# Attention and SwiGLU block on one core: VectorE's weight joins moved to the end of a slot, thresholds and a scaling moved to ScalarE

## The chip, the cores and the metric

One core of a Trainium2 chip. The metric is the time of one execution on the device in microseconds (us). The kernel before took 1633.53 us (median of 3 runs, 1629.41 to 1633.9).

## The reference

```python
# q, k, v: (8 batches, 8 heads, 576, 64);  weights: double precision, 512x1536 twice and 1536x512
scores = scale * q @ k.T
thresh = max(scores, axis=-1) - tau
scores = where(scores >= thresh, scores, -1e9)
attn   = exp(scores - max(scores));  attn /= sum(attn) + 1e-9
x      = (attn @ v) rearranged to (4608, 512)
g      = x @ w_gate
out    = (g * sigmoid(g) * (x @ w_val)) @ w_out
```

## The kernel before

The program is a sequence of *slots*. A slot is one row tile of a pair of heads: scores on TensorE, row maxima (`nm`), threshold (`th`), exponentials, masked products with their sums (`p`), a scaling by the reciprocal sums (`ri`). Slots 1 to 20 are batch one, the rest batches two to eight (`halved`: the same work in halves of 288 columns and a transpose on VectorE). Beside the attention of a slot, `fill` gives TensorE pieces of the feed-forward part from slot 13 on.

The weights come in double precision, in 24 pieces. ScalarE splits a piece into a high and a low half, four VectorE operations put sign, exponent and the high half together, and two GpSimd products add the low half. From the third slot on, each slot joins one piece, so the joins end in the sixth slot of batch two.

```python
def join_weights():
    ...
    nc.vector.tensor_scalar(out=up, in0=up, ..., op0=ALU.min, op1=ALU.max)                        # L169
    nc.vector.tensor_scalar(out=ub, in0=ub, ..., op0=ALU.logical_shift_left, op1=ALU.bitwise_and) # L171
    yield
    nc.vector.scalar_tensor_tensor(out=ub, in0=hi, ..., in1=ub, ...)                              # L174
    nc.vector.tensor_scalar(out=ex.bitcast(U32), in0=ub, ..., op0=ALU.bitwise_and)                # L176
    nc.gpsimd.tensor_tensor(out=lo, in0=lo, in1=ex, op=ALU.mult)                                  # L178
    nc.gpsimd.tensor_tensor(out=up, in0=up, in1=lo, op=ALU.add)                                   # L179

def scores(seg, t):
    ...                                    # matmuls, row maxima nm
    if halved:
        nc.scalar.activation(th[:, 0:m], nm[:, 0:m], AF.Identity, bias=cut, scale=-1.0)           # L300
    else:
        nc.vector.tensor_scalar(out=th[:, 0:m], in0=nm[:, 0:m], ...)                              # L302
    for x in range(m):
        nc.scalar.activation(ps[x], scs[x], AF.Exp, bias=nm[:, x:x + 1])                          # L304
    yield
    ...                                    # transposes of an earlier slot
    for x in range(m):
        nc.vector.scalar_tensor_tensor(out=ps[x], in0=scs[x], scalar=th[:, x:x + 1], in1=ps[x],
                                       op0=ALU.is_ge, op1=ALU.mult, accum_out=...)                # L308
    ...                                    # sums, reciprocal ri (L316)
    yield
    for x in range(m):
        if halved:
            nc.gpsimd.tensor_scalar(out=ps[x], in0=ps[x], scalar1=ri[:, x:x + 1], ...)            # L320
        else:
            nc.scalar.activation(ps[x], ps[x], AF.Copy, scale=ri[:, x:x + 1])                     # L322
    ...

# the slot loop, cut
    go = scores(seg, t); next(go)
    ...
    if n or x:
        weights()            # fetch, first half of the join (L169, L171), split the next piece
    next(go)                 # masked products, sums, reciprocal
    finish_weights()         # second half of the join (L174, L176) and GpSimd's products
    fill(part)
    next(go)                 # scaling of p
    if len(unsig) >= SIG:
        sigmoids()           # three sigmoids, three GpSimd products (L466)
    fill(part)
    ...
    if x == len(seg["tiles"]) - 2 and n + 1 < len(segs):
        prepare(segs[n + 1])                 # transposes of q and k
        fetch_qk(segs[n + 1]["i"] + 1)       # loads of q and k, scaling of q on GpSimd (L220)
```

## Time and profile before

| part of the run | length | what bounds it |
|---|---|---|
| 22 to 103 us, slots 3 to 12, ten joins | 81 us | VectorE |
| 103 to 166 us, rest of batch one | 63 us | TensorE |
| 166 to 240 us, last slot of batch one and six of batch two, last seven joins | 74 us | VectorE |
| from 310 us on | 1320 us | TensorE |

The lines that carry this, with the busy times, are in the prediction below. A line of a group gives source line, engine, operation, tiles and shapes, count, busy us and mean ns of one, and the idle time of the engine in front of it with what ended it. A line of a timeline gives start and duration in us. A record (the stretch of time that the profile gives one instruction) can contain a wait that counts as busy: the same threshold instruction takes 0.61 us in the trace of before and 0.23 us in the first experiment below, at the same place in VectorE's order.

### The profile page before, as it was taken

What the parts mean: (1) busy time and instruction counts of PE and PEld (TensorE: products, weight loads), DVE (VectorE), ACT (ScalarE), POOL (GpSimd) and SP (SyncE); (2) the same over time, 40 slices, a digit from 0 to 9 for tenths busy, and PEclk for the clock granted to TensorE, in tenths of its full rate; (3) what the DMA queues carried; (4) which work ended last, traced back from release to release, by engine and by line L of the source; (5) the groups of instructions that cost most, each with busy time, mean ns of one, the idle gap of its engine ahead of it and who ended that gap; (6) DMA issues with size and microseconds to landing.
All of it is one profiled execution on the core that took longest, in us unless ns stands there. A gap on an engine that the chain in (4) does not pass through costs nothing.

```text
span 1629.5 us, 27646 instructions
## 1 busy us (share of the span) xinstructions
PE 1554.5 (95%) x10192; PEld 835.1 (51%) x10192; DVE 1102.8 (68%) x3680; ACT 571.3 (35%) x1248; POOL 790.9 (49%) x704
## 2 busy tenths in 40 slices
PE   6889779989999999999999999999999999999998
PEld 4555444558545455455545545455545545555453
DVE  7987988777787787777767777767767777601000
ACT  5666532333424323333323423324324323302011
POOL 3543776565455545645545645545555645402011
PEclk9799989999999999999999999999999999999999
DMA  6532221111111111110111111110111110000000
GB/s 160 130 104 98 68 69 37 43 30 37 30 43 30 43 37 22 31 38 20 30 43 37 30 43 36 36 30 20 25 43 37 30 49 16 8 13 0 13 6 20
DMA packets 176342, 66.67 MB, mean 41 GB/s; under 512 B 159568, under 2 KB 159568, under 8 KB 176208
## 3 DMA queue, kind: packets, MB, share of 16 engines
q1 hardware_dynamic: 173328, 55.47, 15.0%
q0 software_dynamic: 2880, 9.44, 1.5%
q8 instruction: 81, 1.33, 0.3%
q14 instruction: 53, 0.43, 0.1%
HBM read 55.44 MB, written 9.44 MB: 40 GB/s over the span
## 4 chain that ended last, share of the span: by engine, by line
PE 79%; DVE 14%; issue 3%; ACT 2%; POOL 1%; DMA 1%; SPq 0%; DVEq 0%; POOLq 0%; ACTq 0%
PE pg L447 20%; PE pv L455 20%; PE po L480 19%; PE sc L268 8%; PE xa L403 8%; DVE p L308 3%; DVE mx L288 2%; DVE p L334 1%; PE sc L273 1%; DVE mx L245 1%; DVE wgv L169 1%; PE xa L375 1%; POOL p L320 1%; DVE nm L298 1%; ACT L304 1%
## 5 line engine op out<-in xcount | busy, mean ns | idle before, releaser
L320 POOL TENSOR_SCALAR p<-p,ri 128x288 f32<-128x288 f32 x504 | 498.4, 1004 | 440.3 <-DVE ri L316 436.5
L447 PE MATMUL pg<-xT,wgv 128*128 128x384 f32 (+1 forms) x1248 | 403.4, 466 | 4.0 <-ACT gt L448 4.0
L455 PE MATMUL pv<-xT,wgv 128*128 128x384 f32 (+1 forms) x1248 | 406.3, 469 | 0.0
L480 PE MATMUL po<-wo,ht 128*128 128x512 f32 x864 | 387.2, 600 | 1.2 <-POOL ht L466 1.2
L455 PEld LDWEIGHTS pv<-xT,wgv 128*128 128x128 f32 x1248 | 231.2, 192 | 152.6 <-issue 17.5
L447 PEld LDWEIGHTS pg<-xT,wgv 128*128 128x128 f32 x1248 | 228.5, 190 | 156.8 <-issue 20.6
L308 DVE SCALAR_TENSOR_TENSOR p<-sc,th,p 128x288 f32<-128x288 f32 (+1 forms) x540 | 257.0, 528 | 39.8 <-ACT p L304 39.4
L480 PEld LDWEIGHTS po<-wo,ht 128*128 128x128 f32 x864 | 160.4, 191 | 207.0 <-issue 195.4
L304 ACT ACTIVATE p<-sc,nm 128x288 f32<-128x288 f32 (+1 forms) x540 | 236.0, 511 | 32.1 <-DVE nm L298 31.5
L288 DVE TENSOR_REDUCE mx<-sc 128x2 f32<-128x576 f32 x252 | 179.5, 749 | 91.7 <-PE sc L268 91.4
L300 ACT ACTIVATE th<-nm,cut 128x4 f32<-128x4 f32 (+1 forms) x140 | 41.6, 297 | 563.2 <-DVE nm L291 563.2
L268 PE MATMUL sc<-kT,qT 64*32 64x288 f32 x4032 | 174.2, 417 | 34.4 <-DVE p L308 34.4
L456 DVE TENSOR_TENSOR ht<-gt,pv 128x384 f32<-128x384 f32 (+1 forms) x156 | 78.3, 510 | 177.9 <-PE pv L455 172.4
L334 DVE STREAM_TRANSPOSE p<-p 128x576 f32<-128x576 f32 x252 | 181.3, 753 | 0.8 <-POOL p L320 0.8
L466 POOL TENSOR_TENSOR ht<-ht,gt 128x768 f32<-128x768 f32 (+1 forms) x78 | 130.4, 1701 | 95.0 <-ACT gt L465 92.4
L268 PEld LDWEIGHTS sc<-kT,qT 64*32 64x32 f32 x4032 | 67.4, 107 | 144.4 <-issue 111.9
L448 ACT COPY gt<-pg 128x384 f32<-128x384 f32 (+1 forms) x156 | 70.6, 458 | 186.0 <-PE pg L447 181.9
L403 PE MATMUL xa<-p,vall 64*64 64x288 f32 x2016 | 132.1, 409 | 2.0 <-ACT gt L448 1.9
L403 PEld LDWEIGHTS xa<-p,vall 64*64 64x64 f32 x2016 | 77.2, 134 | 59.1 <-issue 15.0
L245 DVE TENSOR_REDUCE sums<-sums 32x4 f32<-32x4 f32 (+1 forms) x560 | 83.9, 150 | 10.5
L418 DVE COPY xT<-xa 128x96 f32<-128x96 f32 (+1 forms) x56 | 14.5, 295 | 112.2 <-PE xa L403 112.1
L245 DVE TENSOR_REDUCE mx<-mx 32x4 f32<-32x4 f32 (+1 forms) x560 | 83.1, 148 | 10.4
(72 smaller groups left out, 918.6 us busy)
## 6 DMA issues: line engine op xcount, KB each, us to landing
vall<-in_v_dram SPq DMA_DIRECT2D x112, 144.0 KB, 3.2
qraw<-in_q_dram SPq DMA_DIRECT2D x128, 72.0 KB, 2.3
kraw<-in_k_dram SPq DMA_DIRECT2D x128, 72.0 KB, 2.7
out_dram<-ob POOLq DMA_DIRECT2D x36, 256.0 KB, 2.4
wo<-in_moe_w_gate_dram SPq DMA_DIRECT2D x16, 384.0 KB, 3.5
wo<-in_moe_w_val_dram SPq DMA_DIRECT2D x16, 384.0 KB, 4.0
xT<-in_moe_w_out_dram SPq DMA_DIRECT2D x6, 768.0 KB, 5.8
wo<-in_moe_w_out_dram SPq DMA_DIRECT2D x2, 768.0 KB, 4.4
```

The lines of the kernel that those rows point to most:

```text
L245: nc.vector.tensor_reduce(out=x[g * G:(g + 1) * G, 0:m, 1], in_=x[o * G:(o + 1) * G, 0:m, 0:1], axis=AX.X, op=ALU.max)
L268: nc.tensor.matmul(ps[g * G:(g + 1) * G, u, 0:SH], qT[hs, col + a * G:col + (a + 1) * G], kT[hs, c * SH:(c + 1) * SH], start=True, stop=True)
L288: nc.vector.tensor_reduce(out=mx[:, 2 * x:2 * x + 2, 0], in_=tile_[:, :, 0:SH], axis=AX.X, op=ALU.max, negate=True)
L304: nc.scalar.activation(ps[x], scs[x], AF.Exp, bias=nm[:, x:x + 1])
L308: nc.vector.scalar_tensor_tensor(out=ps[x], in0=scs[x], scalar=th[:, x:x + 1], in1=ps[x], op0=ALU.is_ge, op1=ALU.mult, accum_out=sm[:, x, ...
L320: nc.gpsimd.tensor_scalar(out=ps[x], in0=ps[x], scalar1=ri[:, x:x + 1], scalar2=None, op0=ALU.mult)
L334: nc.vector.transpose(out=p, in_=p)
L403: nc.tensor.matmul(xa[a][h * D:(h + 1) * D, at:at + n * G].rearrange("d (i q) -> d i q", q=G), vr[rs, h, j, :], p[rs, lo:lo + n, j, :], st ...
L447: nc.tensor.matmul(ps[:, 0:n], wgv[:, 0, c, f * P:(f + 1) * P], x[:, c, cs], start=(c == 0), stop=(c == NCC - 1))
L455: nc.tensor.matmul(ps[:, 0:n], wgv[:, 1, c, f * P:(f + 1) * P], x[:, c, cs], start=(c == 0), stop=(c == NCC - 1))
L466: nc.gpsimd.tensor_tensor(out=ht, in0=ht, in1=gt, op=ALU.mult)
L480: nc.tensor.matmul(po, hts[f // 2][:, f % 2, i * P:(i + 1) * P], wo[:, f, :], start=(f == 0), stop=(f == NF - 1))
```

## The change

The intent: all four VectorE operations of a join follow each other at the end of the slot, when GpSimd should have finished the products of the piece before; the thresholds of batch one leave VectorE; and while weights are left, the scaling of p in batch two leaves GpSimd. Blank lines, the removed helpers `weights` and `finish_weights` and the equivalent rewriting of `need` are cut.

```diff
@@ join_weights
                                 op0=ALU.logical_shift_left, op1=ALU.bitwise_and)
-        yield
         nc.vector.scalar_tensor_tensor(out=ub, in0=hi, scalar=0x80000000, in1=ub,
@@ scores
-        else:
-            nc.vector.tensor_scalar(out=th[:, 0:m], in0=nm[:, 0:m], scalar1=-1.0, scalar2=cut, op0=ALU.mult, op1=ALU.add)
         for x in range(m):
+            if not halved:
+                nc.scalar.activation(th[:, x:x + 1], nm[:, x:x + 1], AF.Identity, bias=cut, scale=-1.0)
             nc.scalar.activation(ps[x], scs[x], AF.Exp, bias=nm[:, x:x + 1])
@@
-            if halved:
+            if halved and not split:
                 nc.gpsimd.tensor_scalar(out=ps[x], in0=ps[x], scalar1=ri[:, x:x + 1], scalar2=None, op0=ALU.mult)
             else:
                 nc.scalar.activation(ps[x], ps[x], AF.Copy, scale=ri[:, x:x + 1])
@@ slot loop
+            more = len(split)
             if n or x:
-                weights()
+                fetch_weights(2)
+                split_weights()
             next(go)
-            finish_weights()
+            if more:
+                join_weights()
             fill(part)
```

Line numbers move: L169, L171, L174, L176 become L168, L170, L172, L174; GpSimd's L178, L179 become L176, L177; its q scaling L220 becomes L206, its sigmoid products L466 become L452, its scaling of p L320 becomes L306; the masked product L308 becomes L294.

More of the change, by code (lines that the diff above doesn't have):

```diff
@@ L181, in join_weights @@
         used.discard(place)
-    joining = [iter(())]
-    def weights():
-        for _ in joining[0]:
-            pass
-        fetch_weights(2)
-        joining[0] = join_weights() if split else iter(())
-        next(joining[0], None)
-        split_weights()
-    def finish_weights():
-        for _ in joining[0]:
-            pass
     def need(n):
         while len(joined) < n:
-            weights()
-            finish_weights()
+            fetch_weights(2)
+            if not split:
+                split_weights()
+            join_weights()
+            split_weights()
     def load_qk(i):
@@ L657 @@
                 if prev["i"] % NP == 0:
-                    while wpieces or fetched or split:
-                        weights()
-                    finish_weights()
+                    need(NCC * DFF // TC + DM // ne * DFF // TC)
                     start_batch(prev["i"] // NP)
@@ L663 @@
             part = pace(n, x) / 2
+            more = len(split)
             if n or x:
-                weights()
+                fetch_weights(2)
+                split_weights()
             next(go)
-            finish_weights()
+            if more:
+                join_weights()
             fill(part)
```

## The prediction

> **What bounds the kernel now.** I read the page first: its slices give the shape of the run.
>
> ```profile
> PE   6889779989999999999999999999999999999998
> DVE  7987988777787787777767777767767777601000
> POOL 3543776565455545645545645545555645402011
> PEclk9799989999999999999999999999999999999999
> ```
>
> A slice is 40.7 us. From the eighth slice on TensorE is at 9 tenths, so some 1300 of the 1629.5 us are TensorE work that this change does not touch. Room is only in the first seven slices, 285 us. The windows view, with stretches chosen so that each has one limit, has the columns PE, PEld, DVE, ACT, POOL, clock, DMA share, GB/s:
>
> ```profile
> 22.00:103.00 81.00, 64.61 (x411) 43.35 (x411) 76.11 (x146) 57.52 (x92) 37.80 (x21) 0.83 0.48 124
> 103.00:166.00 63.00, 62.95 (x391) 37.38 (x388) 47.68 (x102) 39.58 (x65) 28.07 (x16) 1.00 0.27 89
> 166.00:240.00 74.00, 54.90 (x380) 29.48 (x379) 70.61 (x176) 31.17 (x60) 53.65 (x38) 0.91 0.30 75
> 240.00:310.00 70.00, 63.24 (x517) 31.37 (x517) 55.52 (x209) 20.57 (x56) 45.10 (x42) 0.98 0.16 33
> ```
>
> So: 22 to 103 us is VectorE's (76.1 of 81 us), 103 to 166 is TensorE's (62.95 of 63), 166 to 240 is VectorE's again (70.6 of 74). The chain of waits agrees: between 22 and 103 us it runs along VectorE with short passes over the score matmuls, and from 166 to 240 along VectorE and one weight transfer. The first stretch is ten slots of the first batch (8.1 us each), each joining one of the 24 pieces of the double-precision weights on VectorE and GpSimd. The third holds the seven last joins, most of them in the slots of batch two (9.2 to 12.9 us each, against 5.2 to 8 us once the weights are done).
>
> Then the groups of instructions of VectorE from 22 to 103 us, shapes kept apart, and the timeline of one slot of that stretch:
>
> ```profile
> L169 DVE TENSOR_SCALAR wgv<-wgv 128x768 f32<-128x768 f32 x10 | 14.0, 1397 | 0.0
> L302 DVE TENSOR_SCALAR th<-nm,cut 128x2 f32<-128x2 f32 x10 | 6.7, 674 | 0.3
> L176 DVE TENSOR_SCALAR wo<-wgv 128x768 uint32<-128x768 uint32 x10 | 5.6, 560 | 0.7
> ```
>
> ```profile
> 61.82 1.81 POOL L178 TENSOR_TENSOR lo<-lo,wo 128x768 f32<-128x768 f32 x1 [4.56 <-DVE wo L176]
> ...
> 63.04 0.61 DVE L302 TENSOR_SCALAR th<-nm,cut 128x2 f32<-128x2 f32 x1
> ...
> 63.71 1.81 POOL L179 TENSOR_TENSOR wgv<-wgv,lo 128x768 f32<-128x768 f32 x1
> ...
> 64.63 1.31 DVE L169 TENSOR_SCALAR wgv<-wgv 128x768 f32<-128x768 f32 x1
> 65.97 0.56 DVE L171 TENSOR_SCALAR wgv<-wgv 128x768 uint32<-128x768 uint32 x1
> ```
>
> This is the key reading. L302 handles two numbers per partition and takes 0.61 us: it ends at 63.65, and GpSimd's L178 ended at 63.63. L169 ends at 65.94, 0.42 us after L179 (65.52); its shortest record in this stretch is 0.54 us, its mean 1.40. L176 and L171, the same size, take 0.56 where GpSimd is idle. VectorE's busy time hides a wait for GpSimd's running instruction.
>
> **What the Trainium skill says.** "SBUF — State Buffer", section "Who interferes with whom": VectorE shares one pair of SBUF ports with GpSimd under an exclusive lock; tensor_scalar in a two-port mode takes it, an operation with two SBUF inputs contends with GpSimd's reads, tensor_reduce never contends, ScalarE never waits. The trace agrees for L302 and L169; the reductions L298 stay at 0.71 us each beside L178. "ScalarE: Activation LUTs", section "What ACT_TABLE_LOAD costs": an activation with a pointer bias takes about 280 ns + 0.833 ns per element and adjacent ones overlap by about 93 ns; here the threshold of batch two (L300, 128x4) has a mean of 297 ns and the next one starts 0.2 us after it. "TensorE: Matmul & The Clock Gate", section "What's actually happening": after an idle window of about 3.4 us TensorE's clock halves; here the score group after a 3.3 us gap at 75.9 us took 2.42 us against 1.94 us after a gap of 1.4 us.
>
> **The change, part by part.** The order of instructions built from both sources: the counts of table loads are equal (46 and 46), TensorE's work is the same, VectorE loses 20 thresholds, ScalarE gains 36 of one column each, and 18 scalings of p move from GpSimd to ScalarE.
>
> *First stretch (ten slots).* Removed: the threshold on VectorE, 6.7 + 0.3 us of idle in front = 7.0. Moved: L169 and L171 go from before the masked products (L308) to behind the reciprocal, next to L174 and L176. GpSimd's pair (3.7 us) then starts at the end of the slot and should be over about 4 us into the next, while the next join starts some 4.4 us after the previous one ended. So L169 should fall to 0.55: 10 x (1.40 - 0.55) = 8.5. Together 15.5 us, 1.55 a slot.
>
> To be taken off: (a) the masked product now follows the maxima with only the copy L381 (0.28 us) between, where th, L169 and L171 used to cover the exponentials. The first exponential is done some 0.1 + 0.2 + 0.74 us after the first maximum, 0.35 us after the second: a wait of 0.1 to 0.3 us a slot, say 2 us in ten. (b) GpSimd's scaling of q (L220, 1.72 us, every third slot, 4 to 6 us after the transposes) used to miss L169 and will now meet the join: about 1.4 us in two or three slots, say 3 us. (c) ScalarE gets 20 x 0.2 = 4 us more in a shorter stretch: (57.5 + 4) / 71 = 87% busy. It then waits for TensorE's transposes only where TensorE is at its slow clock; a further 1 to 2 us. Sum: 15.5 - 2 - 3 - 1.5 = 9 us.
>
> *103 to 166 us.* TensorE has no gap there; VectorE's time is free. I count nothing.
>
> *166 to 240 us.* The join's first two operations hold 11.0 and 7.3 us in seven joins. Unhindered, 0.69 each (the pair at 230.5 us): 18.3 - 9.7 = 8.6 us of waiting for L179, L320 and L466. The scaling L320 (four of 1.03 us) goes to ScalarE, which is only 31.2 of 74 us busy and scales in under 0.5 us, so nothing should stand in the way of the moved join, except at the slot near 166 us, where three products of the sigmoid (L466, 6.5 us) block it in either order: 2 to 3 us of the 8.6 stay. Two slots have no transposes to cover the exponentials: 1.2 us lost. And the last weight piece is late:
>
> ```profile
> 222.63 6.89 DMA xT<-in_moe_w_out_dram
> ```
>
> In the chain it follows the loads of q and k in the same queue, which wait for the transposes that end at 217.9. It lands 11.6 us after those; in the changed order ScalarE, now waiting for it (L155), also holds the scaling and the next exponentials, so the first mask of that slot comes about 15.3 us after the transposes, as it does now (15.2), and the whole join comes behind it: 1 to 1.5 us lost. Sum: 8.6 - 2.5 - 1.2 - 1.3 = 3.6, say 4 us.
>
> **Sum:** 9 + 4 = 13 us. What is gained ahead of 240 us moves all later TensorE work forward: 1633.5 - 13 = 1620.5.
>
> **Rivals.** *ScalarE becomes the bound.* For: 87% of the first stretch, in program order, and the scaling waits for the reciprocal. Against: the reciprocal now comes before the join instead of between its halves. If it holds, slots stay near 7.8 us and the total gain is 5 to 7 us. *TensorE's clock.* If VectorE's shorter slot closes TensorE's gaps, its clock rises (0.83 now) and the passes over L273 and L375 shorten; the first stretch then gains 12 to 14 us and the total 18 to 20. If gaps merely move, TensorE's slow pass (scores, products, transposes, about 8 us at the slow clock) is itself the bound and the gain is under 5. *The lock returns elsewhere.* L178 and L179 now run at the start of the slot; should the joins drift back onto them or L220, half of the 15.5 us returns. *It is hidden anyway.* If the stretch from 103 to 166 us absorbed the gain, the time would not move; against it, TensorE has no gap there, so an earlier start ends it earlier.
>
> **Range and chances.** The two sums have errors of about 4 and 3 us, and the three runs of before spread over 4.5 us. I take 1611 to 1628. Over 2% faster needs 33 us, about half of all TensorE idle in the run (75 us), and more than both stretches' hidden waits (15.5 + 8.6 = 24): 3%. Slower by 2% has no cause in sight: 1%.
>
> **What would show each step right or wrong.** Right: L169's mean near 0.55 us in the first stretch and 0.7 after it, no threshold on VectorE, slots of 7 to 7.3 us, the stretch from the second slot to the first gate matmul 9 us shorter, the first attention product of batch two some 13 us earlier, TensorE from 310 us on unchanged. Wrong: VectorE idle on ScalarE for over 0.4 us a slot (rival one), L169 still above 1 us (the lock), or TensorE idle later on by what was won early.

## The result

The changed kernel took 1619.98 us (median of 4 runs, 1617.98 to 1622.67), the kernel before 1633.19 us (4 runs). The ratio is 0.9925, 95% interval 0.9904 to 0.9946. A ratio is the mean time of one kernel's fast runs over that of the other's of the same rounds, so it is not quite the ratio of the two medians. That is 0.75% faster, clear of noise and within 2%.

The slices of the changed kernel's page (40.4 us each):

```profile
PE   6899779899999999999999999999999999999998
DVE  6977978876888778777766768677767767501000
POOL 3545365555555645646545555645445554402011
PEclk9999889999999999999999999999999999999999
```

TensorE's dip of the fifth and sixth slices is still there; the low clock of the second slice (7 tenths before) is gone. The windows view, cut at the same events as before, not at the same times:

```profile
22.00:91.00 69.00, 57.99 (x424) 38.92 (x423) 64.95 (x136) 59.40 (x112) 38.19 (x21) 0.93 0.56 146
91.00:158.00 67.00, 65.41 (x390) 38.81 (x390) 45.77 (x96) 45.44 (x84) 31.45 (x18) 1.00 0.29 89
158.00:229.00 71.00, 53.79 (x368) 29.72 (x367) 64.30 (x177) 35.12 (x73) 30.91 (x18) 0.86 0.30 73
```

The first stretch took 81 us and takes 69. The third took 74 and takes 71, but the stretch between them grew from 63 to 67: part of that is where the cuts fall, and the milestones below measure it better. The groups of VectorE in the first stretch:

```profile
L172 DVE SCALAR_TENSOR_TENSOR wgv<-wo,wgv 128x768 uint32<-128x768 uint32 x10 | 10.0, 1001 | 0.3
L170 DVE TENSOR_SCALAR wgv<-wgv 128x768 uint32<-128x768 uint32 x10 | 6.5, 650 | 0.3
L168 DVE TENSOR_SCALAR wgv<-wgv 128x768 f32<-128x768 f32 x10 | 6.3, 628 | 0.0
```

L168 is the L169 of before, 1397 ns there and 628 here; the threshold is gone from VectorE. One slot on the timeline, GpSimd and VectorE:

```profile
78.48 1.81 POOL L176 TENSOR_TENSOR lo<-lo,wo 128x768 f32<-128x768 f32 x1 [2.82 <-DVE wo L174]
80.37 1.82 POOL L177 TENSOR_TENSOR wgv<-wgv,lo 128x768 f32<-128x768 f32 x1
...
81.94 0.67 DVE L168 TENSOR_SCALAR wgv<-wgv 128x768 f32<-128x768 f32 x1
82.64 0.56 DVE L170 TENSOR_SCALAR wgv<-wgv 128x768 uint32<-128x768 uint32 x1
```

GpSimd's pair ends at 82.19, so L168 meets only its last quarter of a microsecond and loses some 0.1 us; the rest of the pair now lies beside operations of VectorE that do not wait for it.

To find where the gain lies I read four distances from each trace. **A to B**: first row maximum of slot 3 to that of slot 13, the ten joins of the first stretch. **B to C**: from there to the first score matmuls of batch two. **C to D**: to the first row maximum of batch two. **D to E**: to the first row maximum of the seventh slot of batch two, the slots with the last six joins.

| run | A to B | B to C | C to D | D to E | sum |
|---|---|---|---|---|---|
| before | 80.7 | 67.3 | 2.7 | 65.2 | 215.9 |
| changed | 68.9 | 67.6 | 5.3 | 62.5 | 204.3 |
| changed, second trace | 69.0 | 67.6 | 5.3 | 64.0 | 205.8 |

From E to the end are 1391.2 us before and 1389.6 and 1390.8 us after: nothing is given back. So the first stretch gives 11.8 us, and the third, from C to E, 0.1 us (65.2 + 2.7 against 62.5 + 5.3) in one trace and a loss of 1.4 in the other.

### The profile page after: what moved, and what is told of

Its sections match the earlier page's. It is cut to its first block, busy times and chain, and to the rows that moved or that the text cites. A ratio compares the mean times of both kernels' runs of the same rounds, so it can differ in the third digit from the quotient of the medians.

```text
span 1616.2 us, 27669 instructions
## 1 busy us (share of the span) xinstructions
PE 1547.4 (96%) x10192; PEld 831.2 (51%) x10192; DVE 1082.5 (67%) x3660; ACT 583.5 (36%) x1302; POOL 771.3 (48%) x686
## 4 chain that ended last, share of the span: by engine, by line
PE 77%; DVE 13%; ACT 4%; issue 3%; POOL 1%; DMA 1%; SPq 1%; DVEq 0%; POOLq 0%; ACTq 0%
PE pg L433 20%; PE pv L441 20%; PE po L466 19%; PE sc L254 8%; PE xa L389 8%; DVE p L294 3%; DVE mx L274 2%; DVE p L320 1%; ACT p L290 1%; DVE mx L231 1%; POOL p L306 1%; ACT L290 1%; SPq L203 1%; DVE sums L231 1%; POOL ht L452 0%
## 5 line engine op out<-in xcount | busy, mean ns | idle before, releaser
L306 POOL TENSOR_SCALAR p<-p,ri 128x288 f32<-128x288 f32 x486 | 479.0, 1001 | 439.2 <-DVE ri L302 435.1
L466 PE MATMUL po<-wo,ht 128*128 128x512 f32 x864 | 386.4, 599 | 1.2 <-POOL ht L452 1.2
L294 DVE SCALAR_TENSOR_TENSOR p<-sc,th,p 128x288 f32<-128x288 f32 (+1 forms) x540 | 258.3, 529 | 49.8 <-ACT p L290 48.6
L466 PEld LDWEIGHTS po<-wo,ht 128*128 128x128 f32 x864 | 160.1, 190 | 206.5 <-issue 194.6
L320 DVE STREAM_TRANSPOSE p<-p 128x576 f32<-128x576 f32 x252 | 181.3, 754 | 0.8 <-POOL p L306 0.8
L452 POOL TENSOR_TENSOR ht<-ht,gt 128x768 f32<-128x768 f32 (+1 forms) x78 | 129.5, 1688 | 95.0 <-ACT gt L451 92.4
L389 PEld LDWEIGHTS xa<-p,vall 64*64 64x64 f32 x2016 | 77.3, 134 | 59.4 <-issue 15.1
```

The costliest lines, as they stand in the source:

```text
L320: nc.vector.transpose(out=p, in_=p)
L389: nc.tensor.matmul(xa[a][h * D:(h + 1) * D, at:at + n * G].rearrange("d (i q) -> d i q", q=G), vr[rs, h, j, :], p[rs, lo:lo + n, j, :], st ...
L452: nc.gpsimd.tensor_tensor(out=ht, in0=ht, in1=gt, op=ALU.mult)
L466: nc.tensor.matmul(po, hts[f // 2][:, f % 2, i * P:(i + 1) * P], wo[:, f, :], start=(f == 0), stop=(f == NF - 1))
```

## The experiments

Theory: the long L169 and L302 are waits for GpSimd's running products, so it is the place of the operations that matters, not their number. Rival: the operations cost this much by themselves, and the gain is VectorE's smaller load. A second question is why the third stretch gave nothing, although its joins lost their waits.

### GpSimd's two weight products taken away

```diff
-        nc.gpsimd.tensor_tensor(out=lo, in0=lo, in1=ex, op=ALU.mult)
-        nc.gpsimd.tensor_tensor(out=up, in0=up, in1=lo, op=ALU.add)
```

On the kernel before; the low halves of the weights are missing (the result still passed the comparison).

> The kernel before without GpSimd's two products per weight piece (the low halves of the weights are left out on purpose, so the result is off in the last bits or fails). VectorE's order is untouched. Lock theory: the long L169 (1.40 us in the first stretch) and L302 (0.67 us) are waits for those products, so they fall to 0.55 and about 0.25 us, the first stretch shortens by 11 to 13 us (first score group of batch two at 170.4 us before, now 157 to 160 us) and the time by 13 to 20 us. Rival (these instructions are slow by themselves, and the change gained by moving load from VectorE to ScalarE): both keep their durations and the time stays within 3 us.

Measured: 1608.46 us, ratio 0.9845 (0.983 to 0.9859). VectorE's groups in the first stretch, A to B:

```profile
L169 DVE TENSOR_SCALAR wgv<-wgv 128x768 f32<-128x768 f32 x10 | 5.5, 550 | 0.0
L300 DVE TENSOR_SCALAR th<-nm,cut 128x2 f32<-128x2 f32 x10 | 2.3, 228 | 0.4
```

The same two instructions at the same place in VectorE's order (L300 is L302 of before) now take 0.55 and 0.23 us; A to B is 66.9 us, 13.8 shorter, and C comes at 155.7 us, a little earlier than expected. The time fell by 24 us, more than the expected 13 to 20: D to E lost another 5.4 us and the part behind E 3.5. The rival falls: without GpSimd's products there is nothing to wait for. It also shows about what placing alone could win at most in the first stretch, 13.8 us; the change got 11.8, and that with the thresholds' own 2.3 us taken off VectorE as well.

Not every threshold waits. In the trace of before, those of one column (128x1, in the half-size slots) take 0.21 us also while L179 is running, as at 115.11 us, where those of two columns wait until GpSimd's instruction has ended. So the wait depends on the shape of VectorE's operation too.

### The thresholds alone

```diff
-        else:
-            nc.vector.tensor_scalar(out=th[:, 0:m], ...)
+            if not halved:
+                nc.scalar.activation(th[:, x:x + 1], nm[:, x:x + 1], AF.Identity, bias=cut, scale=-1.0)
```

> The kernel before with only the thresholds of the first batch on ScalarE. Lock theory: L169 takes the place of L302 between GpSimd's two products, and the wait for the second product falls on L171 instead, so L171's mean in the first stretch rises from 0.56 to above 1.2 us, and the first score group of batch two comes only 2 to 5 us earlier (165.5 to 168.5). Rival (load): 7 us earlier, the sum of L302's records, with L169 and L171 unchanged.

Measured: 1629.18 us, ratio 0.9971 (0.9955 to 0.9988).

```profile
L171 DVE TENSOR_SCALAR wgv<-wgv 128x768 uint32<-128x768 uint32 x10 | 13.1, 1305 | 0.3
L169 DVE TENSOR_SCALAR wgv<-wgv 128x768 f32<-128x768 f32 x10 | 9.5, 950 | 0.0
L381 DVE COPY xT<-xa 128x128 f32<-128x128 f32 x10 | 2.8, 284 | 4.6 <-PE xa L379 4.6
```

The wait moved as expected: L171 rose from 560 to 1305 ns (L169 fell from 1397 to 950), and A to B is 78.8 us, only 1.9 shorter although 6.7 us of records left VectorE. Not all of that is GpSimd: VectorE's wait for TensorE at the copy of the attention product (L381) rose from 2.4 to 4.6 us. C came at 171.4 us, a miss of the expected 165.5 to 168.5. Most of that is not the change: from slot 13 to slot 14 this run needed 13.9 us and the one before 11.2 (without this, C would have come at about 168.7). The scaling-only run below, which has the same instructions as before up to there, needed 14.1. In that trace TensorE's score group at the slow place took 2.99 us and its attention products 1.97, against 1.95 and 1.09 in the trace of before. That is TensorE's clock: the windows view gives 1.00 from slot 13 to 14 before, 0.84 in this run and 0.82 in the scaling-only run. Ahead of the slow score group TensorE had stood idle for 2.6 us in this run and 3.0 in the scaling-only run, for 0.8 before. It differs between executions with the same instructions and is worth 2.9 us. So I compare stretches, not arrival times.

### The join alone

```diff
-        yield            # in join_weights
...
+            more = len(split)
-                weights()
+                fetch_weights(2)
+                split_weights()
             next(go)
-            finish_weights()
+            if more:
+                join_weights()
```

> The kernel before with only the join moved behind the reciprocal. Lock theory: L169's mean in the first stretch falls to 0.55 to 0.65 us, L302 still waits 0.6 us for the first product; the first score group of batch two comes 6 to 9 us earlier (161.5 to 164.5). Rival (load): VectorE has the same instructions, so no gain. At the slot of the first sigmoids (166 us before) the join should meet the products L466 and lose 2 us, as it does in the changed kernel.

Measured: 1622.86 us, ratio 0.9933 (0.9918 to 0.9948).

```profile
L288 DVE TENSOR_SCALAR th<-nm,cut 128x2 f32<-128x2 f32 x10 | 6.7, 673 | 0.4
L168 DVE TENSOR_SCALAR wgv<-wgv 128x768 f32<-128x768 f32 x10 | 6.6, 659 | 0.0
```

As expected: the join's wait is gone, the threshold (L288) still waits for the first product, and A to B is 73.2 us, 7.6 shorter. VectorE has exactly the instructions of before, so this gain is placing alone; TensorE's granted clock was 0.84 from A to B, practically that of before (0.83), so it is not the clock either. C came at 164.8 us, 0.3 later than expected; slot 13 to 14 took 12.8 us here. C to D is 5.3 us, as in the changed kernel, so the loss there belongs to the join. Thresholds alone give 1.9 us, the join alone 7.6, both together 11.8: each leaves the other operation to catch a product.

### The scaling alone

```diff
-            if halved:
+            if halved and not split:
                 nc.gpsimd.tensor_scalar(out=ps[x], ...)
```

> The kernel before with only the scaling of p on ScalarE while weights are left. The step of the prediction: the join's first two operations wait for L320, so 3 us or more of the stretch from 166 to 240 us go. Rival, from the traces: they wait for L179, the product of the piece before, which starts when VectorE has finished that piece whatever L320 does; then L169's mean in batch two stays at 1.4 us or more and the time within 1.5 us of before.

Measured: 1633.85 us, ratio 1.0003 (0.9988 to 1.0018). VectorE's group from 173 to 243 us, first the kernel before, then this run:

```profile
L169 DVE TENSOR_SCALAR wo<-wo 128x768 f32<-128x768 f32 x6 | 9.5, 1590 | 1.1 <-ACT wo L155 1.1
```

```profile
L169 DVE TENSOR_SCALAR wo<-wo 128x768 f32<-128x768 f32 x6 | 9.5, 1588 | 1.8 <-ACT wo L155 1.8
```

The mean differs by 2 ns, so none of the wait was for the scaling L320. The rival named in the expectation holds: L169 waited for GpSimd's products, in the trace of before for L178 in the first slot of batch two and for L179 in the next four (its record ends 0.55 us after theirs).

### The changed kernel with the scaling back on GpSimd

```diff
-            if halved and not split:
+            if halved:
```

> The changed kernel with the scaling of p in batch two back on GpSimd. If the scaling on ScalarE was a gain (the prediction's view), the six slots of batch two that still join weights (62.5 us from the first to the seventh row maximum of batch two in the changed kernel) get 2 us or more longer. If it is a loss, as the join-only run hints (61.4 us there), they get about 1 us shorter, at the slot of the late last piece, and the time stays within 2 us of the changed kernel's 1620.

Measured: 1619.24 us, ratio 0.9933 (0.9916 to 0.995). D to E was 63.3 us, neither 2 us longer nor clearly 1 us shorter than the changed kernel's 62.5 and 64.0, so by that distance the run is inconclusive. Split by slots it is not. The first five slots of batch two take 49.96 us here and 49.95 in the join-only run (scaling on GpSimd), and 50.11 and 49.97 in the two traces of the changed kernel (on ScalarE). The scaling makes no difference there. The sixth slot holds the rest, and it follows the transfer of the last weight piece:

| run | scaling | that transfer | sixth slot |
|---|---|---|---|
| join only | GpSimd | 5.70 us | 11.49 us |
| this run | GpSimd | 7.54 us | 13.29 us |
| changed | ScalarE | 5.83 us | 12.36 us |
| changed, second trace | ScalarE | 7.33 us | 13.99 us |

At equal transfer, the scaling on ScalarE costs that slot 0.7 to 0.9 us, by these two pairs of single traces.

### Sigmoid products one per slot

```diff
...                                   # multiply(n), new: issues up to n of the waiting products
 def sigmoids():
     for _, gt, ht in unsig:
         nc.scalar.activation(gt, gt, AF.Sigmoid)
-        nc.gpsimd.tensor_tensor(out=ht, in0=ht, in1=gt, op=ALU.mult)
+        products_.append((gt, ht))
     unsig.clear()
+    if not split:
+        multiply(len(products_))
...
             if more:
                 join_weights()
+            multiply(1)
```

> The changed kernel with the three sigmoid products L452 (5.5 us in a row on GpSimd) issued one per slot behind the weight products, instead of together before the last join of batch one. Theory: that join met them and lost 2.3 us on L168, L170 and L172, so the three fall to 0.66, 0.69 and 0.96 us there and the distance from the first score group of batch two to its first row maximum falls from 5.3 to about 2.6 us; no later join gets over 0.3 us longer. The time falls by 2 to 3 us against the changed kernel. Rival: the wait only moves to the three joins that follow, and nothing is gained.

The join of the last slot of batch one, in the kernel before (the exponentials L304 end at 168.77, so the wait in L171 keeps the masked product L308 back by no more than 0.6 us):

```profile
166.91 6.46 POOL L466 TENSOR_TENSOR ht<-ht,gt 128x768 f32<-128x768 f32 x3
167.53 1.92 DVE L171 TENSOR_SCALAR wo<-wo 128x768 uint32<-128x768 uint32 x1
168.03 0.74 ACT L304 ACTIVATE p<-sc,nm 128x576 f32<-128x576 f32 x1
169.37 0.80 DVE L308 SCALAR_TENSOR_TENSOR p<-sc,th,p 128x576 f32<-128x576 f32 x1
```

in the changed kernel:

```profile
155.56 5.55 POOL L452 TENSOR_TENSOR ht<-ht,gt 128x768 f32<-128x768 f32 x3
...
158.13 1.55 DVE L168 TENSOR_SCALAR wo<-wo 128x768 f32<-128x768 f32 x1
159.72 1.94 DVE L170 TENSOR_SCALAR wo<-wo 128x768 uint32<-128x768 uint32 x1
```

and here:

```profile
157.23 0.67 DVE L168 TENSOR_SCALAR wo<-wo 128x768 f32<-128x768 f32 x1
157.94 0.95 DVE L170 TENSOR_SCALAR wo<-wo 128x768 uint32<-128x768 uint32 x1
```

Measured: 1618.88 us, ratio 0.9924 (0.9909 to 0.9939); C to D is 3.3 us instead of 5.3, not quite the expected 2.6. A part of the rest is the scaling of q (L206), which now meets L170 (0.95 instead of 0.69 us); and the whole join still lies behind the masked products, where half of it lay ahead of them before. The five slots that follow got longer by 0.2 us at most (10.09, 10.09, 9.64, 11.45, 9.06 us against 10.10, 10.08, 9.64, 11.45, 8.84), so the rival falls. Two microseconds are as much as the times of single runs scatter; the milestones show the gain, the ratio alone does not.

### The last weight piece fetched first

```diff
             if x == len(seg["tiles"]) - 2 and n + 1 < len(segs):
+                if n == 2 * NP:
+                    fetch_weights(1)
                 prepare(segs[n + 1])
                 fetch_qk(segs[n + 1]["i"] + 1)
```

> The changed kernel with the last weight piece's transfer issued ahead of the loads of q and k in the same queue. Theory: ScalarE's 7.9 us wait for that piece shrinks by some 4 us, VectorE's idle of 2.1 us before the masked products of that slot goes, and the slot (12.4 us) becomes 10.2 to 10.5; time 2 us less than the changed kernel. Rival: the slot is held by VectorE's own work or the loads of q and k, now later, hold the next slot, and nothing is gained.

In the changed kernel VectorE waits for ScalarE before the masked products of that slot:

```profile
219.98 0.52 DVE L294 SCALAR_TENSOR_TENSOR p<-sc,th,p 128x288 f32<-128x288 f32 x1 [2.08 <-ACT p L290]
```

ScalarE's waits for the weight transfers (line, what it waited for: us in total, times, longest), changed kernel, then this run:

```profile
ACT wo L155 <- DMA xT<-in_moe_w_out_dram: 10.2, 2, 7.9
```

```profile
ACT wo L155 <- DMA xT<-in_moe_w_out_dram: 4.5, 2, 2.3
```

Measured: 1617.41 us, ratio 0.9922 (0.9905 to 0.994). The sixth slot of batch two took 10.17 us instead of 12.36 (13.99 in the other trace), and D to E 60.0 us. The loads of q and k, now behind, delayed nothing: the slot after it took 13.36 us, as in the changed kernel. So the late piece held that slot.

### Both mended, and the scaling once more

The two edits together:

> The changed kernel with the products spread and the last piece fetched early. The two losses lie in different slots, so they should add: 4 to 5 us off the changed kernel's 1620, so about 1615.

Measured: 1615.18 us, ratio 0.9905 (0.989 to 0.9921). C to D 3.6 us, D to E 60.0 us: the two losses add. It was repeated with the changed kernel, five rounds each, together with a version of it that scales p on GpSimd again:

> The changed kernel itself, beside the next two on one chip. Ratio to before 0.992 to 0.993; the distances between its milestones in the first 230 us repeat within 0.3 us, except where TensorE's clock or a transfer differs from run to run (some 3 us at the first gate product, some 2 us at the last weight piece).

> The mended kernel (products spread, last piece early) once more with more rounds: 3 to 5 us below the changed kernel of the same call, ratio to before 0.9895 to 0.991.

> The mended kernel with the scaling of p back on GpSimd. With the products spread, GpSimd has 3.7 + 1.8 + 4.2 = 9.7 us of work in slots of about 10 us, so joins should now meet the scaling or the product: if a running scaling blocks VectorE as the prediction thought, L168 and L170 grow by 1 us a slot in three slots and the time is 2 to 4 us above the mended kernel's; if it does not block (as the timeline of before hints, where L171 ran in 0.69 us beside L320), the time is within 1 us of it.

| kernel | median | ratio to before | 95% interval |
|---|---|---|---|
| changed | 1620.53 us | 0.9932 | 0.9919 to 0.9945 |
| mended | 1615.06 us | 0.9896 | 0.9881 to 0.9911 |
| mended, scaling on GpSimd | 1616.39 us | 0.9904 | 0.9887 to 0.992 |

The mended kernel is 5.5 us below the changed one, a little more than the 3 to 5 expected, and clear of noise. The last version is 1.3 us above it, between the two forecasts (within 1 us, 2 to 4 us) and within the noise; the traces decide. In them, 2.8 us apart, it takes 0.55 us more from D to E (60.55 against 60.0), in slots whose join met a scaling, and 1.4 us more from slot 13 to 14, where the clock differs. So it answers what a running scaling does to a join. Its timeline in the second slot of batch two:

```profile
179.13 4.62 POOL L306 TENSOR_SCALAR p<-p,ri 128x288 f32<-128x288 f32 x4
...
180.21 0.96 DVE L168 TENSOR_SCALAR wo<-wo 128x768 f32<-128x768 f32 x1
181.20 0.69 DVE L170 TENSOR_SCALAR wo<-wo 128x768 uint32<-128x768 uint32 x1
```

The four scalings run until 183.75, and the join passes beside them: L168 loses 0.3 us, L170 and the rest nothing. The scalings themselves get longer, 1.06, 1.26 and 1.36 us where an undisturbed one takes 1.00. Four scalings in a row block almost nothing; three products in a row (the lines of the changed kernel above) cost the same two operations 2.1 us.

What no run settles: why TensorE's clock comes up differently at slot 13 from one execution to the next, and why the last transfer takes 5.7 us in some executions and 7.5 in others. The Trainium skill ("TensorE: Matmul & The Clock Gate", "What's actually happening") says that the window in which TensorE's activity is judged runs freely, so that the same kernel meets a different number of slow matmuls from run to run; the gaps and clocks above fit that, but no run here tests it. No experiment here controls either, and the loss at the sixth slot of the second trace rests on the latter.

## Why the prediction was right

The time (1620.5 predicted, 1619.98 measured) was nearly exact, and that is partly luck: the first stretch gave 2.8 us more than forecast and the third 3.9 us less.

- **The bound and the lock.** Right. The records of L169 and L302 held waits for GpSimd's products (first experiment), and what was won early was passed on to the end. One reading is off, without effect: the reductions L298 take 0.75 us each by their group, not 0.71; beside L178 they are no longer than elsewhere.
- **First stretch, 9 us predicted, 11.8 measured.** The removed time was nearly right (L169's records lost 7.7 us, 8.5 predicted: the next join starts 3.6 us after the one before, not 4.4, and so meets the end of GpSimd's pair in six of ten slots); the three deductions were too large. (a) The wait for the exponentials cost 1.1 us in ten slots (VectorE idle in front of L294), not 2. (b) The scaling of q meets the join as foreseen, but does not hold it to its end: three collisions cost about 0.4 to 0.5 us each (L170 took 1.06 us at 48 us and L172 1.38 us at 70 us), 1.3 us together and not 3. (c) No further wait for ScalarE appeared, though it is busy 59.4 of 69 us; the thresholds took 0.28 to 0.30 us each and the exponential behind each started 0.2 us after it, which agrees with "ScalarE: Activation LUTs", "What ACT_TABLE_LOAD costs". One gain was not in the sum: VectorE's wait for TensorE at the copy of the attention product fell from 2.4 to 0.5 us. TensorE's granted clock rose from 0.83 to 0.93 in this stretch, as the clock rival has it, but the join-only run has the same short wait (0.5 us) at 0.84, so the clock is not shown to be the cause. The terms do not add up exactly to 11.8, since records on VectorE overlap by some 0.1 us.
- **103 to 166 us, nothing.** Right: 67.3 and 67.6 us from B to C.
- **Third stretch, 4 us predicted, 0.1 measured in the trace that belongs to the result.** This step failed, though the waits were sized rightly: L169 and L171 held 18.3 us in the seven joins, L168 and L170 hold 11.9, 6.4 less where 6.1 was forecast. What failed are two of the losses set against them. The first is the join that meets the sigmoid products: the prediction let "2 to 3 us of the 8.6 stay", as if nothing changed for them. But before, that wait lay ahead of the masked products, where VectorE would have waited for the exponentials for all but 0.6 us of it anyway (the table loads of ScalarE are in that slot); behind the reciprocal nothing covers it. C to D went from 2.7 to 5.3 us, so the gain shrank by another 2.6 us, of which spreading the products returned 2.0. The second is the cover of the exponentials together with the late piece: VectorE waited 4.0 us for ScalarE in these slots (0.95, 1.01 and 2.08), where 1.2 plus 1.3 had been set aside. Together these are 6.6 us, as much as the joins won. The reading of the late piece was right, and fetching it early returned 2.2 us.
- **The scaling L320 among the things waited for.** Wrong. The prediction listed it beside L179 and L466; the scaling-only run left L169 at 1588 ns (1590 before). The trace of before had it already: in five joins of batch two L171 ran in 0.69 us, as where GpSimd is idle, while L320 was running.
- **ScalarE as the bound; the gain hidden later.** Neither came: no slot of the first stretch waited for ScalarE above 0.2 us, and the part from E to the end kept its length within 1.6 us.

## What to carry to other kernels

An operation of VectorE whose record is several times that of its equals, with no idle in front of it, may be waiting inside its record for GpSimd: compare its end with the end of GpSimd's instruction, and move it to where GpSimd is idle before thinking of making it cheaper. Moving one waiting operation away only hands the wait to the next of its kind, so move all of them, and do not move a hidden wait to a place where nothing covers it. When total times scatter by 3 us and parts are worth 2, read distances between fixed events of the traces.

## What the Trainium skill lacked or had wrong

- "SBUF — State Buffer", "Who interferes with whom", says that whoever comes first has the shared pair for its whole instruction. That agrees here with GpSimd's tensor_tensor: L169 ended 0.42 us after L179, its own shortest time being 0.54. It does not agree with GpSimd's tensor_scalar: four of them ran for 4.62 us while L168 lost 0.3 us and L170 nothing, and the scaling of q (1.72 us) delayed one VectorE operation by 0.5 us at most. That is as far as GpSimd's records, whose spans are rough, can show it. The page does not tell the two apart.
- No page says how such a wait shows in a profile: it lies inside VectorE's busy record (0.61 us for two numbers per partition, 0.23 without GpSimd's products) and in no idle time or wait.
